# Whole-row loads cast by GpSimd, and single tail banks, in a block-sparse attention and feed-forward kernel

## The chip, the cores and the metric

The kernel runs on one core of a Trainium2 chip. The metric is the device time of one execution in microseconds (us); lower is better. The core has a matrix engine (TensorE, PE in the profile, with its weight loads as PEld), VectorE (DVE), ScalarE (ACT), GpSimd (POOL) and SyncE (SP), and 16 DMA engines that all queues share. SBUF is the memory that the engines work in, PSUM the one that TensorE writes, divided into banks. The granted clock is the share of TensorE's full clock that the profile shows. Kernels are compared with the kernel before as it ran in the same rounds on the same chip.

## The reference, cut to what matters

```python
# q, k, v: [4 batches, 8 heads, 768 tokens, 64] fp32; sampled_blocks: [24, 3]
scores = (q @ k.T) / sqrt(64)
mask   = |block_i - block_j| <= 1, or a first/last block, or a sampled block   # blocks of 32 tokens
attn   = softmax(where(mask, scores, -1e9))
x      = (attn @ v) -> [3072, 512]
xn     = x / sqrt(mean(x*x) + 1e-6) * rms_g
g      = xn @ w_gate                  # [3072, 1536]
out    = (g * sigmoid(g) * (xn @ w_val)) @ w_out      # [3072, 512] fp32
```

## The kernel before

Work is cut into 12 chunks of 256 tokens, three to a batch. Each chunk has an attention part (scores `s_`, exponential and mask product `pt`, output product `o_`) and a feed-forward part (`gp`, `vp` or the tail's `gv`, then `th`, `uu`, `hp`, `yp`). A small list scheduler in the kernel's Python (`Plan`) decides in which order each engine's instructions are written. It is static: once written, an engine runs its instructions in that order, and a time such as `after=60.0` is a hint for the ordering, never a wait on the chip.

K, Q and V of batches 1 to 3 are loaded by GpSimd in slices of one column group, cast from fp32 to bf16 on the way, and laid out so that a DMA transpose can take them:

```python
def load_c(b, i, c):                                   # 128 KB, c = 0..5, K and Q
    ...
    nc.gpsimd.dma_start(
        out=flat[:, c * DM:(c + 1) * DM].rearrange("p (h d) -> p h d", h=H),
        in_=src[b, :, :, c * D:(c + 1) * D])
...                                                    # in the plan, for each c:
nc.gpsimd.dma_start(out=va[b % 2][:, :, c, 0:D], in_=vv4[b, :, :, c, :])
```

GpSimd also computes the normaliser `rs` of each chunk, on which VectorE's scaling of `x` waits, and from there the transposes `xn`, which SyncE issues as DMA transposes for most chunks:

```python
def rstd(ch):
    rs = work.tile([P, 2], FP32, name="rs", tag="rs")
    nc.gpsimd.tensor_scalar(out=rs, in0=mss[ch], scalar1=1e-6, scalar2=None, op0=ALU.add)
    nc.gpsimd.tensor_tensor(out=rs, in0=rs, in1=nhalf, op=ALU.pow)
...
def x_dma(ch, qt):
    ...
    nc.sync.dma_start_transpose(out=xns[ch][:, :, qt * P:(qt + 1) * P], in_=x2s[ch, qt])
```

The mask is applied by a VectorE product whose two inputs both lie in SBUF:

```python
def mask_(t):
    ...
    nc.vector.tensor_tensor(out=pv, in0=pv,
        in1=m.unsqueeze(1).to_broadcast([P, 2, 2 * CQ]), op=ALU.mult)
```

At the end, when no scores are left, the feed-forward borrows the scores' PSUM tiles. One tile of two banks then holds gate and value of a pair together:

```python
def product(w, u, fp, name, half):
    if WIDE(u, fp):
        if (u, fp) not in wide:
            wide[u, fp] = ps_s.tile([P, 2, 512], FP32, name="gv", tag="s")
        pp = wide[u, fp][:, 0 if name == "gp" else 1]
    ...
```

The softmax here doesn't subtract the row's maximum and nothing guards it: scores larger than these inputs give would overflow.

Of the kernel before, what the change touches and what calls it, by code (L numbers as in the profile page):

```python
# [8 lines left out]
FP32 = mybir.dt.float32  # L9
# [6 lines left out]
HOLD = 41.978  # L16
SOFT = 0.0051
LEAD = 29
SPEED = 1.0
PRIO = {'av': 4, 'e': 6, 'g': -5, 'h': -6, 'm': 16, 'mk': -2, 'mt': 4, 'on': -2, 'rs': 21, 's': 3, 'sc': 2, 'sq': 18, 't': 4, 'th': -1, 'uu': -5, 'v': 4, 'x': -2, 'xt': -6, 'y': 7, 'yo': 7}  # L20


class Plan:
# [24 lines left out]
    def run(self, log=None):  # L48
        self.free = free = {e: 0.0 for e in ("PE", "ACT", "DVE", "POOL", "SP")}
        free.update(DVE=4.6, POOL=4.5, ACT=1.5)  # L50
# [4 lines left out]
        dma_free = 14.4  # L55
# [77 lines left out]
def kernel(  # L133
# [13 lines left out]
    P = 128  # L147
# [22 lines left out]
    ps_s = ctx.enter_context(tc.tile_pool(name="ps_s", bufs=2, space=bass.MemoryType.PSUM))  # L170
    ps_o = ctx.enter_context(tc.tile_pool(name="ps_o", bufs=1, space=bass.MemoryType.PSUM))
    ps_f = ctx.enter_context(tc.tile_pool(name="ps_f", bufs=3, space=bass.MemoryType.PSUM))

# [12 lines left out]
    for name, n in (("s", 2), ("o", 1), ("f", 3), ("pt", 4), ("x1", 2), ("x2", 3), ("xn", 3),  # L186
                    ("hp", 2), ("th", 3), ("uu", 3), ("yo", 3), ("qk", 2), ("raw", 1)):
        plan.pool(name, n)
# [26 lines left out]
    def load_c(b, i, c):  # L215
        raw_tiles(b)
        src, t = ((qv, qraw), (kv, kraw))[i]
        flat = t[b].rearrange("p h w -> p (h w)")
        nc.gpsimd.dma_start(  # L219
            out=flat[:, c * DM:(c + 1) * DM].rearrange("p (h d) -> p h d", h=H),  # L220
            in_=src[b, :, :, c * D:(c + 1) * D])
# [10 lines left out]
    load_q(2, 8, 0, 2)  # L232
    jb = const.tile([32, 2 * 32 + 1], I32, name="jb")
    nc.gpsimd.iota(jb[:, 0:32], pattern=[[1, 32]], base=0, channel_multiplier=0)
    nc.gpsimd.iota(jb[:, 32:64], pattern=[[1, 32]], base=0, channel_multiplier=-1)
    nc.gpsimd.iota(jb[:, 64:65], pattern=[[1, 1]], base=0, channel_multiplier=1)
    load_k(2, 4)
    load_k(4, 8)
# [10 lines left out]
    vraw = raw.tile([P, H, NC * D], FP32, name="vraw")  # L249
    for lo in (0, 4):  # L250
        nc.gpsimd.memset(vraw[:, lo:lo + 4, 0:1], 0.0)
        nc.sync.dma_start(out=vraw[:, lo:lo + 4, :], in_=vv[0, :, lo:lo + 4, :])
    gB = const.tile([P, DM], FP32, name="gB")
    nc.sync.dma_start(
        out=gB, in_=moe_rms_g.rearrange("(o f) -> o f", o=1).to_broadcast([P, DM]))
    warm = fbank("warm")
    for _ in range(8):
        nc.tensor.matmul(out=warm, lhsT=idle[:, 0:P], rhs=idle, start=True, stop=True)
# [15 lines left out]
    for lo in (0, 64):  # L274
        nc.vector.tensor_copy(out=R[:, lo:lo + 32], in_=ident[0:32, 0:32])
    jbf = const.tile([32, 2 * 32 + 1], FP32, name="jbf")
    nc.vector.tensor_copy(out=jbf, in_=jb)
    near = const.tile([32, 32], FP32, name="near")
    nc.vector.tensor_tensor(
        out=near, in0=jbf[:, 32:64], in1=jbf[:, 32:64], op=ALU.mult)  # L280
    edge = const.tile([32, 2], FP32, name="edge")
    nc.vector.tensor_scalar(
        out=edge[:, 0:1], in0=jbf[:, 64:65], scalar1=0.0, scalar2=None, op0=ALU.is_equal)
    nc.vector.scalar_tensor_tensor(
        out=edge[:, 1:2], in0=jbf[:, 64:65], scalar=NB - 1.0, in1=edge[:, 0:1],
        op0=ALU.is_equal, op1=ALU.max)
    nc.vector.tensor_scalar(
        out=Bm[:, 0:NB], in0=near[:, 0:NB], scalar1=1.0, scalar2=edge[:, 1:2],
        op0=ALU.is_le, op1=ALU.max)
    nc.vector.memset(Bm[:, 0:1], 1.0)  # L290
    nc.vector.memset(Bm[:, NB - 1:NB], 1.0)
    samp_f = const.tile([32, NRND], FP32, name="samp_f")
    nc.vector.tensor_copy(out=samp_f[0:NB, :], in_=samp_i[0:NB, 0:2 * NRND:2])
    for r in range(NRND):
        nc.vector.scalar_tensor_tensor(
            out=Bm[0:NB, 0:NB], in0=jbf[0:NB, 0:NB], scalar=samp_f[0:NB, r:r + 1],
            in1=Bm[0:NB, 0:NB], op0=ALU.is_equal, op1=ALU.max)
    nc.vector.tensor_copy(out=Bm[0:NB, 64:64 + NB], in_=Bm[0:NB, 0:NB])
# [14 lines left out]
    K_AT = {0: 0.0, 1: 7.4, 2: 10.5, 3: 10.5}  # L313
    V_AT = (12.6, 14.7)

    def cast_first(e, i):
        src, dst = ((qf, qraw[0][:, 0:2, 0:2 * D]), (kf, kraw[0][:, 0:2, :]))[i]
        (nc.scalar.copy if e == "ACT" else nc.vector.tensor_copy)(out=dst, in_=src)

    plan.add("cast0", {"DVE": dve1(256), "ACT": act(256)}, lambda e: cast_first(e, 0), after=3.2,  # L320
             prio=0)
    plan.add("cast1", {"DVE": 0.55, "ACT": act(768)}, lambda e: cast_first(e, 1), after=3.4,
             prio=0)
    plan.add("qrest", {"POOL": 0.8}, lambda e: load_q(0, 8, 2, 6), dma=4.2, prio=0, after=4.5)
    for half in range(2):
        for nm, dst, src in (("wg", wg, wgv), ("wv", wv, wvv)):
            plan.add(
                f"{nm}{half}", {"POOL": 0.8},
                lambda e, d=dst, s=src, h=half: nc.gpsimd.dma_start(
                    out=d[:, :, h * HF:(h + 1) * HF], in_=s[:, :, h * HF:(h + 1) * HF]),  # L330
                dma=3.8, prio=half, after=5.0,
                deps=[">wg0", ">wv0"] if half else [">qrest"])
    plan.add("wo", {"POOL": 0.9}, lambda e: nc.gpsimd.dma_start(
        out=wo, in_=moe_w_out.rearrange("(c p) f -> p c f", p=P)), dma=7.5, prio=2, deps=[">wg1", ">wv1"])
    for i in range(2):
        plan.add(f"one{i}", {"POOL": 0.2}, lambda e, i=i: nc.gpsimd.memset(
            va[i][:, :, :, D:D + 2], 1.0), prio=1, after=7.0)
    for h2 in range(2):
        plan.add(f"va0_{h2}", {"POOL": 1.6}, lambda e, h2=h2: nc.gpsimd.tensor_copy(
            out=va[0][:, 4 * h2:4 * h2 + 4, :, 0:D],  # L340
            in_=vraw[:, 4 * h2:4 * h2 + 4, :].rearrange("p h (c d) -> p h c d", c=NC)),
            deps=["one0"], prio=2 + h2, after=V_AT[h2])

# [25 lines left out]
    TP = [(pr, i, c0, c1) for pr in range(NP) for i, c0, c1 in ((0, 0, 2), (1, 0, NC), (0, 2, NC))]  # L369
    for pr, i, c0, c1 in TP:  # L370
        n = f"{pr}_{i}_{c0}"
        plan.add(f"t{n}", {"PE": 0.04 * 2 * (c1 - c0)},
                 lambda e, pr=pr, i=i, c0=c0, c1=c1: transposes(pr, i, c0, c1),
                 acq=["f"], mode="t", prio=4 if c0 else 0, after=0.0 if c0 else K_AT[pr], lat=0.2,
                 deps=["qrest"] if c0 else [f"cast{i}"] if pr == 0 else [])
        plan.add(f"e{n}", {"DVE": dve2(P * (c1 - c0)) + 0.05, "ACT": act(P * (c1 - c0))},
                 lambda e, pr=pr, i=i, c0=c0, c1=c1: evac_qk(e, pr, i, c0, c1),
                 deps=[f"t{n}"], rel=["f"], prio=0)
# [61 lines left out]
    for i in range(2):  # L440
        plan.add(f"kr{i}", {"PE": 0.3}, lambda e, i=i: key_rows(i), acq=["f"], mode="m",
                 prio=0, after=3.6, lat=0.2)
        plan.add(f"kc{i}", {"DVE": dve1(384), "ACT": act(384)}, lambda e, i=i: key_copy(e, i),
                 deps=[f"kr{i}"], rel=["f"], prio=0)
    for ic in range(NIC):
        plan.add(f"mq{ic}", {"PE": 0.3}, lambda e, ic=ic: mask_query(ic), acq=["f"], mode="m",
                 prio=0, after=QAT[ic], lat=0.2)
# [12 lines left out]
    for b in range(1, B):  # L460
        plan.add(f"rawq{b}", {"SP": 0.0}, lambda e: None, acq=["raw"], lat=0.0, prio=0,
                 deps=[f"raw{b - 1}"] + ([">wo"] if b == 1 else []))
        prev = None
        for i, c0, c1 in KT:
            for c in range(c0, c1):
                plan.add(f"l{b}_{i}_{c}", {"POOL": 0.9},
                         lambda e, b=b, c=c, i=i: load_c(b, i, c),
                         deps=[f"rawq{b}"] + ([">" + prev] if prev else []), dma=2.05, prio=20 + b)
                prev = f"l{b}_{i}_{c}"
        for c in range(NC):  # L470
            plan.add(f"vl{b}_{c}", {"POOL": 0.9}, lambda e, b=b, c=c: nc.gpsimd.dma_start(  # L471
                out=va[b % 2][:, :, c, 0:D], in_=vv4[b, :, :, c, :]),
                deps=[">" + prev] + ([f"one{b % 2}"] if b == 1 else [])
                + ([f"av{(b - 2) * NIC + NIC - 1}_{NP - 1}_2"] if b >= 2 else []),
                dma=2.05, prio=20 + b)
# [3 lines left out]
        for i, c0, c1 in KT:  # L479
            plan.add(f"dt{b}_{i}_{c0}", {"SP": 0.3 + 1.25 * (c1 - c0)},  # L480
                     lambda e, b=b, i=i, c0=c0, c1=c1: transposes_dma(b, i, c0, c1),
                     deps=[f"qk{b}"] + ([">" + prev] if prev else []) + [f"l{b}_{i}_{c}" for c in range(c0, c1)], lat=2.5, prio=1)
# [130 lines left out]
    for run in runs:  # L613
        i = TILES.index(run[0])
        deps = set()
        for ch, pr, j2 in run:
            b, ic = divmod(ch, NIC)
            if b == 0:
                deps |= {f"e{pr}_0_{0 if ic == 0 else 2}", f"e{pr}_1_0"}
# [17 lines left out]
    for ch, pr, j2 in TILES:  # L637
# [13 lines left out]
        if b == 0:  # L651
            deps.append(f"va0_{pr // 2}")
        else:
            deps += [f"vl{b}_{c}" for c in (2 * j2, 2 * j2 + 1)]
# [42 lines left out]
    def product(w, u, fp, name, half):  # L697
        if WIDE(u, fp):
            if (u, fp) not in wide:
                wide[u, fp] = ps_s.tile([P, 2, 512], FP32, name="gv", tag="s")  # L700
            pp = wide[u, fp][:, 0 if name == "gp" else 1]
# [54 lines left out]
    for u in range(NCH):  # L756
        for f in range(NFP):
# [4 lines left out]
            elif u:  # L762
                deps.append(f">v{u - 1}_{NFP - 1}f")
            if f == AHEAD and u:
# [3 lines left out]
                     deps=deps, acq=["s" if WIDE(u, f) else "f"], **w)  # L768
# [5 lines left out]
                     deps=[f"th{u}_{f}"], acq=["uu"], rel=["th"] if WIDE(u, f) else ["f", "th"], prio=2)  # L774
            plan.add(f"v{u}_{f}a", {"PE": pe(CQ, KC)}, lambda e, u=u, f=f: product(wv, u, f, "vp", 0),
                     deps=[f">g{u}_{f}", f"wv{half}"], acq=[] if WIDE(u, f) else ["f"], **w)
# [4 lines left out]
                     acq=["hp"] if f == 0 else [], rel=["s" if WIDE(u, f) else "f", "uu"], prio=2)  # L781
# [53 lines left out]
```

## Time and profile before

| | before |
|---|---|
| median time (3 runs) | 319.47 us (319.18 to 319.92) |
| span of the profiled run, granted TensorE clock | 318.3 us, 0.983 |
| TensorE / VectorE / ScalarE / GpSimd busy | 294.2 / 229.4 / 213.2 / 70.9 us |

The page's table of busy time, kernel before: engine, busy us, share of the span, and the number of instructions.

```profile
PE 294.2 (92%) x3337; PEld 206.2 (65%) x3359; DVE 229.4 (72%) x439; ACT 213.2 (67%) x300; POOL 70.9 (22%) x102
```

TensorE is busy 92% of the time, so time can be won only where it stands still or runs slowly. The waits of TensorE before: what waited, which line's result it waited for, us in total, how often, and the longest.

```profile
PE mp L426 <- DVE uu L719: 7.4, 1, 7.4
PE gv L709 <- ACT th L715: 5.5, 8, 0.7
```

There are two kinds of hole: one wait of 7.4 us, and eight short ones in the tail, where the value matmuls stop for the tanh of the gate that shares their tile. VectorE, for whose `uu` the long one waits, itself waited up to 7.9 us for `rs` from GpSimd (VectorE's waits before, same columns):

```profile
DVE x L582 <- POOL rs L577: 14.7, 10, 7.9
```

The timeline of GpSimd tells the reason. The columns are start, duration, engine, line, operation, output and input, count, and in brackets how long the engine idled before and what ended that.

```profile
43.26 1.74 POOL L219 DMA_DIRECT2D qb<-in_q_dram  x2 [6.46 <-DMA wo<-in_moe_w_out_dram]
45.43 2.63 POOL L219 DMA_DIRECT2D qb<-in_q_dram  x3 [0.43 <-issue]
48.03 4.40 POOL L471 DMA_DIRECT2D va<-in_v_dram  x5
52.64 0.88 POOL L471 DMA_DIRECT2D va<-in_v_dram  x1 [0.20 <-issue]
53.59 0.22 POOL L575 TENSOR_SCALAR rs<-ms 128x2 f32<-128x2 f32 x1
```

GpSimd stood 6.46 us for the load of `wo` to land, then issued five `qb` and six `va` loads, and only then came to `rs`. The stage table of the kernel before gives the busy us of each engine in stretches of 4 us, then the granted clock of TensorE, the share of the DMA engines and GB/s.

```profile
core 0: us, PE busy (x) PEld busy (x) DVE busy (x) ACT busy (x) POOL busy (x), PEclk, DMA share, GB/s
48.00:52.00 4.00, 0.64 (x6) 0.42 (x5) 0.00 (x0) 1.34 (x2) 4.00 (x6) 0.93 2.45 155
52.00:56.00 4.00, 0.00 (x0) 0.00 (x0) 1.36 (x3) 0.00 (x0) 2.25 (x4) 0.50 2.81 148
56.00:60.00 4.00, 3.96 (x27) 2.62 (x28) 3.19 (x7) 2.51 (x3) 0.00 (x0) 0.50 1.03 97
```

TensorE did nothing from 52 to 56 us, and then worked at half the clock. The Trainium skill ("TensorE: Matmul & The Clock Gate", Part 1: The HAM clock gate) says that an idle window of about 3.4 us halves the clock and a busy one of the same length restores it; this trace agrees roughly: the wait began near 48.6 us, the clock was 0.50 from about 51.5 us, some 3 us later, and until about 61.7 us, 5.7 us after work had resumed at 56.0.

Two more lines of the kernel before serve for comparison later: the mask products as a group (busy us, mean ns of one, idle time before them), and the landing times of the `xn` transposes issued between 60 and 125 us.

```profile
L532 DVE TENSOR_TENSOR pt<-pt,Mk 128x1024 bf16<-128x1024 bf16 x132 | 87.2, 684 | 6.0 <-ACT pt L525 6.0
```

```profile
DMA to landing us min/median/max: 2.4/5.3/6.7
```

### The profile page before, as it was taken

Reading aid. Unit: us, or ns where it says so; the run is one execution under the profiler, and the core shown is the slowest. Engines: PE = TensorE matmul, PEld = TensorE weight load, DVE = VectorE, ACT = ScalarE, POOL = GpSimd, SP = SyncE. Lnnn points to the kernel's source line nnn. Section 1 sums busy time; section 2 is a strip of 40 time slices with the busy share of each in tenths; the row PEclk is TensorE's granted clock in tenths of the full one; section 3 lists DMA queues with packets and bytes.
Section 4 is the critical chain, followed back from the end, with each engine's and each line's share of the span. In section 5 each row is a group of like instructions: output and inputs, shape, how many; then the busy total and the mean of one; then the engine's idle time right before and its main releaser. Section 6 shows DMA issues by size and latency. Waiting matters only on the chain.

```text
span 318.3 us, 7937 instructions
## 1 busy us (share of the span) xinstructions
PE 294.2 (92%) x3337; PEld 206.2 (65%) x3359; DVE 229.4 (72%) x439; ACT 213.2 (67%) x300; POOL 70.9 (22%) x102
## 2 busy tenths in 40 slices
PE   7998991999899999999999999999999999997975
PEld 2675780577658667757867757848758758675552
DVE  6239981786859978987986977887978969745151
ACT  4789991465778887888876976967867866332221
POOL 9326258007094109570010000100100100100000
PEclk9999997699999999999999999999999999999999
DMA  7999999869999989999921020020020020010101
GB/s 124 252 233 210 208 163 153 103 104 111 136 102 149 132 150 114 149 111 131 166 50 52 2 69 35 0 68 35 0 69 35 16 81 7 30 38 0 68 0 66
DMA packets 97655, 29.61 MB, mean 93 GB/s; under 512 B 87380, under 2 KB 94548, under 8 KB 97620
## 3 DMA queue, kind: packets, MB, share of 16 engines
q0 software_dynamic: 62448, 13.11, 50.9%
q1 hardware_dynamic: 34756, 15.74, 25.5%
q8 instruction: 26, 0.43, 0.6%
q10 hardware_dynamic: 416, 0.26, 0.3%
q14 instruction: 9, 0.07, 0.1%
HBM read 28.57 MB, written 6.29 MB: 110 GB/s over the span
## 4 chain that ended last, share of the span: by engine, by line
PE 68%; DMA 11%; POOL 7%; DVE 6%; ACT 4%; issue 3%; POOLq 0%; ACTq 0%; DVEq 0%
PE yp L736 17%; PE gp L709 14%; PE vp L709 14%; DMA wo<-in_moe_w_out_dram 11%; PE gv L709 5%; ACT junk L569 2%; POOL va L471 2%; ACT th L715 2%; DVE hp L726 2%; DVE x L582 2%; POOL qb L219 1%; DVE uu L719 1%; DVE pt L532 1%; POOL rs L577 1%; POOL qb L209 1%
## 5 line engine op out<-in xcount | busy, mean ns | idle before, releaser
L532 DVE TENSOR_TENSOR pt<-pt,Mk 128x1024 bf16<-128x1024 bf16 x132 | 87.2, 684 | 6.0 <-ACT pt L525 6.0
L709 PE MATMUL vp<-xn,wv 128*128 128x256 bf16 x512 | 69.8, 275 | 0.0
L736 PE MATMUL yp<-wo,hp 128*128 128x512 bf16 x266 | 67.6, 382 | 1.3 <-DVE hp L726 0.2
L709 PE MATMUL gp<-xn,wg 128*128 128x256 bf16 x512 | 66.4, 273 | 1.1 <-DVE hp L726 1.1
L709 PEld LDWEIGHTS <-wg 128*128 128x128 bf16 x576 | 56.1, 98 | 10.3 <-issue 1.7
L709 PEld LDWEIGHTS <-wv 128*128 128x128 bf16 x576 | 52.8, 98 | 13.9 <-issue 8.3
L715 ACT ACTIVATE th<-gp 128x512 bf16<-128x512 f32 x64 | 38.3, 598 | 28.0 <-PE gp L709 26.2
L546 PEld LDWEIGHTS <-pt 128*128 128x128 bf16 x1152 | 43.3, 98 | 19.6 <-issue 9.2
L719 DVE SCALAR_TENSOR_TENSOR uu<-th,gp 128x512 bf16<-128x512 bf16 x64 | 43.6, 682 | 14.5 <-ACT th L715 14.1
L726 DVE TENSOR_TENSOR hp<-uu,vp 128x512 bf16<-128x512 bf16 x64 | 43.6, 682 | 4.0 <-PE vp L709 1.9
L736 PEld LDWEIGHTS <-hp 128*128 128x128 bf16 x288 | 25.9, 98 | 25.8 <-issue 3.2
L575 POOL TENSOR_SCALAR rs<-ms 128x2 f32<-128x2 f32 x12 | 2.8, 230 | 168.1 <-ACT junk L569 168.0
L510 PEld LDWEIGHTS <-qkT 64*128 64x128 bf16 x576 | 23.9, 96 | 20.7 <-issue 16.4
L753 ACT ACTIVATE yo<-yp 128x512 f32<-128x512 f32 x23 | 13.8, 598 | 24.6 <-PE yp L736 24.5
L582 DVE SCALAR_TENSOR_TENSOR x<-x,rs,gB 128x512 bf16<-128x512 f32 x24 | 17.6, 748 | 14.8 <-POOL rs L577 14.7
L219 POOL DMA_DIRECT2D qb<-in_q_dram x18 | 15.8, 911 | 19.9 <-DMA qkT<-qb 9.3
L471 POOL DMA_DIRECT2D va<-in_v_dram x18 | 15.9, 923 | 4.7 <-PE o__2395 L546 4.5
L219 POOL DMA_DIRECT2D kb<-in_k_dram x18 | 16.0, 912 | 1.4 <-DMA wg<-in_moe_w_gate_dram 1.4
L719 DVE SCALAR_TENSOR_TENSOR uu<-th,gv 128x512 bf16<-128x512 bf16 x8 | 5.5, 687 | 14.9 <-PE gv L709 14.9
L569 ACT ACTIVATE junk<-x 128x512 bf16<-128x512 f32 x24 | 15.0, 628 | 1.9 <-DVE x L560 1.8
L709 PE MATMUL gv<-xn,wv 128*128 128x256 bf16 x64 | 9.6, 272 | 5.5 <-ACT th L715 5.5
L715 ACT ACTIVATE th<-gv 128x512 bf16<-128x512 f32 x8 | 4.8, 597 | 14.3 <-PE gv L709 14.3
(509 smaller groups left out, 386.2 us busy)
## 6 DMA issues: line engine op xcount, KB each, us to landing
out_dram<-yo SPq DMA_DIRECT2D x23, 256.0 KB, 2.1
kb<-in_k_dram POOLq DMA_DIRECT2D x18, 128.0 KB, 7.6
qb<-in_q_dram POOLq DMA_DIRECT2D x18, 128.0 KB, 6.9
va<-in_v_dram POOLq DMA_DIRECT2D x18, 128.0 KB, 6.8
vraw<-in_v_dram SPq DMA_DIRECT2D x2, 768.0 KB, 12.0
wg<-in_moe_w_gate_dram POOLq DMA_DIRECT2D x2, 768.0 KB, 21.4
wv<-in_moe_w_val_dram POOLq DMA_DIRECT2D x2, 768.0 KB, 24.4
wo<-in_moe_w_out_dram POOLq DMA_DIRECT2D x1, 1536.0 KB, 34.2
```

The costliest lines, as they stand in the source:

```text
L219: nc.gpsimd.dma_start(out=flat[:, c * DM:(c + 1) * DM].rearrange("p (h d) -> p h d", h=H), in_=src[b, :, :, c * D:(c + 1) * D])
L471: plan.add(f"vl{b}_{c}", {"POOL": 0.9}, lambda e, b=b, c=c: nc.gpsimd.dma_start(out=va[b % 2][:, :, c, 0:D], in_=vv4[b, :, :, c, :]), deps ...
L510: nc.tensor.matmul(out=s_[:, e, jj * CQ:(jj + 1) * CQ], lhsT=x[rows, 1, 2 * j2 + jj, pr, :], rhs=x[rows, 0, 2 * ic:2 * ic + 2, pr, :], sta ...
L532: nc.vector.tensor_tensor(out=pv, in0=pv, in1=m.unsqueeze(1).to_broadcast([P, 2, 2 * CQ]), op=ALU.mult)
L546: nc.tensor.matmul(out=o_[:, qt, e, 0:D + 1], lhsT=pt[:, j2, e, jj * CQ + qt * P:jj * CQ + (qt + 1) * P], rhs=va[(ch // NIC) % 2][:, 2 * p ...
L569: nc.scalar.activation(out=junk, in_=x1s[ch][:, qt].rearrange("p h d -> p (h d)"), func=AF.Square, scale=float(DM) ** -0.5, accum_out=mss[ ...
L582: nc.vector.scalar_tensor_tensor(out=x2s[ch, qt], in0=x1s[ch][:, qt].rearrange("p h d -> p (h d)"), scalar=mss[ch][:, qt:qt + 1], in1=gB, ...
L709: nc.tensor.matmul(out=pp[:, half * CQ:(half + 1) * CQ], lhsT=w[:, c, f * P:(f + 1) * P], rhs=xns[u][:, c, :], start=(c == 0), stop=(c == ...
L715: nc.scalar.activation(out=ths[u, fp], in_=gst[u, fp, "gp"], func=AF.Tanh, scale=0.5)
L719: nc.vector.scalar_tensor_tensor(out=uus[u, fp], in0=ths.pop((u, fp)), scalar=1.0, in1=gst.pop((u, fp, "gp")), op0=ALU.add, op1=ALU.mult)
L726: nc.vector.tensor_tensor(out=hps[u][:, 2 * fp:2 * fp + 2, :].rearrange("p f t -> p (f t)"), in0=uus.pop((u, fp)), in1=gst.pop((u, fp, "vp ...
L736: nc.tensor.matmul(out=yst[u, t], lhsT=hps[u][:, f, t * P:(t + 1) * P], rhs=wo[:, f, :], start=(f == 0), stop=(f == NF - 1))
```

## The change

The intent is to shorten GpSimd's queue and to free the tail:

- K, Q and V of batches 1 to 3 are loaded as whole rows, one plain fp32 load of 1.5 MB each, into a staging tile. GpSimd then casts them from there into the layout for the DMA transposes. So 54 casting loads become nine plain loads and 48 casts. (Batch 0's V goes the same way, in two loads and four casts.)
- V of batch 0 is loaded in the same GpSimd queue, before the rest of Q and the weights.
- The tail takes four single banks from a new pool in place of the two double tiles.
- The scheduler's constants and priorities were tuned again for the new plan, and the first steps rearranged (seven warm-up matmuls in place of eight, the mask's preparation put into the plan).

```diff
-    def load_c(b, i, c):
+    def load_stage(b, i):
+        stages[b, i] = raw.tile([P, H, NC * D], FP32, name="stage", tag="stage", bufs=2)
+        if b:
+            nc.gpsimd.dma_start(out=stages[b, i], in_=(qv, kv, vv)[i][b])
+
+    def cast_c(b, i, c):
         raw_tiles(b)
...
-        nc.gpsimd.dma_start(
+        nc.gpsimd.tensor_copy(
             out=flat[:, c * DM:(c + 1) * DM].rearrange("p (h d) -> p h d", h=H),
-            in_=src[b, :, :, c * D:(c + 1) * D])
+            in_=stages[b, i][:, :, c * D:(c + 1) * D])
+
+    def cast_v(b, pr):
+        nc.gpsimd.tensor_copy(
+            out=va[b % 2][:, 2 * pr:2 * pr + 2, :, 0:D],
+            in_=stages[b, 2][:, 2 * pr:2 * pr + 2, :].rearrange("p h (c d) -> p h c d", c=NC))
...
+        for i in (1, 0, 2):                            # K, Q, V of batch b
+            swdge(f"l{b}_{i}", lambda b=b, i=i: load_stage(b, i), 4.4,
+                  [">wo"] if (b, i) == (1, 1) else [">" + last], 20 + b, acq=["stage"],
+                  after=0.0 if b == 1 else 60.0 * b - 20.0)
...
     def product(w, u, fp, name, half):
-        if WIDE(u, fp):
-            if (u, fp) not in wide:
-                wide[u, fp] = ps_s.tile([P, 2, 512], FP32, name="gv", tag="s")
-            pp = wide[u, fp][:, 0 if name == "gp" else 1]
+        if WIDE(u, fp) and half == 0:
+            if not wide:
+                s_stack.close()
+                wide[0] = ctx.enter_context(
+                    tc.tile_pool(name="ps_t", bufs=4, space=bass.MemoryType.PSUM))
+            pp = wide[0].tile([P, 512], FP32, name="gv", tag="t")
```

## The prediction

> **What bounds it now.** TensorE: the busy table has it busy 294 of 318.3 us, VectorE 229, ScalarE 213, GpSimd 71. From 90 to 270 us the stage table shows TensorE 98-100% busy at full clock; chunks there repeat every 22.8 us, which is what their matmuls take. Time can only come from holes:
>
> 1. *The hole at 48.65 us.* The waits view gives TensorE one wait of 7.4 us. The timeline names the cause: GpSimd's in-order queue. The normaliser's `rs` for chunk 1 (its squares were ready at 46.0) runs at 53.6, behind six `qb` and six `va` load issues of 0.88 us each, which themselves waited 6.5 us for the `wo` load to land at 43.3. VectorE waits 7.9 us for `rs`. Then the granted clock is 0.50 from about 51.5 to 61.5 us. The Trainium skill ("TensorE: Matmul & The Clock Gate", Part 1) says about 3.4 us of idleness halves the clock; this trace agrees. Some 5.5 us of matmuls ran at half rate: 2.5-3 us more. Hole total about 10 us.
> 2. *The tail.* Eight waits of 0.69 us, `gv` for ScalarE `th`: gate and value share one two-bank tile, so the value matmuls stop until the tanh of the gate has ended. 5.5 us.
> 3. *Start.* To the first FFN matmul at 29.65 us, about 3 us more than its matmuls; ScalarE's exponentials (0.91 us apart) bind there.
> 4. *End:* last output, about 4 us.
>
> **What the change does.** Per later batch, 18 casting loads of 128 KB (0.91 us of GpSimd each, 16.4 us) become 3 plain whole-row loads (2.7 us) plus 16 GpSimd casts. The 128x1536 cast took 1.47 us, so I estimate 0.5 us for 128x512 and 0.75 us for 128x768: 9 us a batch. In the order of the changed kernel, chunk 1's `rs` stands before all casts of batch 1, and only the K and Q loads stand before it, whose queue slots freed early. So hole 1 and its half clock go: about -10 us. The tail takes four single banks: gate and value no longer block one another, and the bank of the pair after next is free before it is wanted (gate end + 0.8 + 0.7 us against 2.6 us): -5.5 us.
>
> Loads: `wo` should still land near 43; it read 3.1 MB in 7.4 us, so K of batch 1 lands at about 47.5, Q at 52, casts end near 57, transposes near 60. Summing matmul durations in the new order, the first scores of batch 1 are wanted near 65 us: just in time. V before the weights helps the first output products by 1-3 us, but the exponentials bind: -0.5 us or so.
>
> **Cost.** "SBUF — State Buffer" (two separate sides) says a GpSimd operation and a VectorE one with two SBUF inputs exclude each other. The mask products (132 of 0.66 us) are such; no run here shows it yet. 27 us of casts may delay VectorE by up to 12 us in sum; with 14% slack on VectorE from 100 to 180 us I allow TensorE +2 us.
>
> Sum: 319.5 - 10 - 5.5 - 0.5 + 2 = 303.5 us; range 298.5 to 309. Chances: faster by over 2% 0.95, within 2% 0.04, slower 0.01.
>
> **Signs.** Right: no TensorE wait above 3 us and clock 1.00 after 15 us; no `gv` wait for `th`; GpSimd issues 9 batch loads; chunk period still 22.8 us. Casts of `kb` clearly over 0.5 us beside mask products, or masks over 0.68 us: the port lock is real.
>
> **What would make it wrong.** Batch 1's K/Q arriving after 65 us, so that the fixed order stalls TensorE there; casts stretched to 1 us or more; `rs` of chunk 2 or 7 held behind casts that wait for a load; the lengthened period.

## The result, and the profile after

| | before (same rounds) | after |
|---|---|---|
| median time (4 runs each) | 319.7 us (319.18 to 320.01) | 314.89 us (314.4 to 316.11) |
| ratio after to before | | 0.9857, 95% interval 0.9825 to 0.9889 |
| span of the profiled run, clock | 318.3 us, 0.983 | 312.6 us, 0.989 |

A ratio here is the mean time of one kernel's fast runs over that of the other's of the same rounds, so it is not quite the ratio of the medians quoted beside it. Where a gain or a cost is told in us below, it is a difference of two such ratios times 319.5 us, which takes out small differences between the rounds. By that measure the change gained 4.6 us, and 16 had been forecast.

The waits of TensorE after, in the same columns as before:

```profile
PE gp L757 <- DMA xn<-x: 4.6, 1, 4.6
PE o__1059 L592 <- DVE pt L578: 3.1, 2, 2.7
PE o__342 L592 <- POOL va L234: 1.9, 1, 1.9
PE o__2062 L592 <- DVE pt L578: 1.4, 1, 1.4
```

Both old kinds of wait are gone: no `mp` wait of 7 us, no `gv` wait. In their place stand waits that the kernel before did not have: 4.6 us for a DMA transpose, and 3.1, 1.9 and 1.4 us for a mask product, a V cast and another mask product. The timeline of GpSimd after shows that the cure of the old hole worked as planned.

```profile
46.52 0.22 POOL L621 TENSOR_SCALAR rs<-ms 128x2 f32<-128x2 f32 x1 [20.78 <-ACT junk L615]
...
47.48 4.78 POOL L229 CAST kb<-stage 128x512 bf16<-128x512 f32 x6
52.56 0.95 POOL L224 DMA_DIRECT2D stage<-in_v_dram  x1 [0.30 <-POOL kb L229]
53.51 3.84 POOL L229 CAST qb<-stage 128x512 bf16<-128x512 f32 x6
```

`rs` of chunk 1 now runs at 46.52 us instead of 53.59. But it is followed by casts, twelve in nearly unbroken runs. The timeline of VectorE after, beside the second of these runs:

```profile
53.51 5.00 DVE L578 TENSOR_TENSOR pt<-pt,Mk 128x1024 bf16<-128x1024 bf16 x3
```

Three mask products took 5.00 us there; one of them alone took 3.38 us, and 0.68 us is what a mask product takes undisturbed. This one was the first of the three; it started in the same instant as the first `qb` cast. The next stage table is of the kernel after, with the columns of the one before.

```profile
52.00:56.00 4.00, 2.24 (x30) 1.21 (x27) 4.00 (x4) 2.51 (x3) 3.70 (x7) 1.00 0.77 154
56.00:60.00 4.00, 3.05 (x19) 1.45 (x20) 3.96 (x7) 0.00 (x1) 1.36 (x2) 0.57 0.99 346
```

From 52 to 56 us VectorE was busy all of the time, waiting inside its mask products, and TensorE 2.24 us. The half clock came back as well, for a shorter time: 0.57 on average from 56 to 60 us. As groups, the mask products and the casts after, in the columns of the group view:

```profile
L578 DVE TENSOR_TENSOR pt<-pt,Mk 128x1024 bf16<-128x1024 bf16 x132 | 94.5, 742 | 3.9 <-ACT pt L571 3.8
...
L234 POOL CAST va<-stage 128x768 bf16<-128x768 f32 x16 | 14.3, 928 | 15.8 <-DMA stage<-in_v_dram 15.8
L229 POOL CAST kb<-stage 128x512 bf16<-128x512 f32 x18 | 13.9, 812 | 5.8 <-DMA stage<-in_k_dram 5.8
...
L229 POOL CAST qb<-stage 128x512 bf16<-128x512 f32 x18 | 12.4, 734 | 0.0
```

The mask products grew by 7.3 us in sum. The casts, which take 0.61 us (128x512) where nothing disturbs them, average 0.81 and 0.73 us: each side delays the other.

The second new hole, of 4.6 us, ends at 107.86 us. Two whole-row loads of batch 2 were issued just beside the two `xn` transposes of chunk 3, which SyncE issued at 93.90 and 96.02. This is GpSimd's timeline after:

```profile
93.01 0.95 POOL L224 DMA_DIRECT2D stage<-in_k_dram  x1
93.96 0.88 POOL L224 DMA_DIRECT2D stage<-in_q_dram  x1
```

And this is the view of the DMA queues of the kernel after from 92 to 108 us. The first line gives the packets of the loads' queue, its MB and the share of the 16 engines' time; the others give issues, KB each, and median us from issue to landing.

```profile
q0 software_dynamic: 736, 3.15, 63.6%
...
stage<-in_k_dram POOLq DMA_DIRECT2D x1, 1536.0 KB, 7.8
stage<-in_q_dram POOLq DMA_DIRECT2D x1, 1536.0 KB, 12.4
out_dram<-yo SPq DMA_DIRECT2D x1, 256.0 KB, 12.1
xn<-x SPq DMA_TRANSPOSE x2, 13.1
```

The first of the two transposes took 13.1 us to land (the profile shows no landing of the second; TensorE's wait for both ended 11.8 us after its issue). 2.4 us is the shortest in this trace, and an output store beside them took 12.1 us. In the kernel before, the `xn` transposes issued between 60 and 125 us landed in at most 6.7 us, this longest one beside slice loads of K; chunk 3's own, issued as the last V slices landed, took 3.5 and 2.4 us. But small pieces do not make every transpose quick. From 92 to 108 us of the kernel before, two K transposes, each three times as large as one of `xn`, ran beside slice loads with packets of 1.34 MB / 10607 = 0.13 KB:

```profile
q0 software_dynamic: 10607, 1.34, 141.9%
...
qkT<-kb SPq DMA_TRANSPOSE x2, 12.9
```

A load packet of the kernel after averages 3.15 MB / 736 = 4.3 KB, and the 16 engines moved up to 419 GB/s in this window, 26 GB/s each, so a load packet holds an engine for about 0.16 us. A pair of transposes and a store alone, in a quiet stretch, show 1104 packets under 512 B, some 34 for each transpose and engine. An estimate from these numbers: if each small packet lets one large one pass, 34 x 0.16 = 5.5 us for a transpose and 11 us for a pair, near the 13.1 measured. The Trainium skill ("DMA: Bandwidth & Descriptors", Queues, rings and completion order) states that each DMA engine goes round its queues packet by packet; this estimate agrees in size with the trace, which doesn't show single turns, and d2_slices below does not bear it out.

How far each kernel is ahead can be read from when a given piece of work starts:

| start of | before | after | lead |
|---|---|---|---|
| first feed-forward matmul | 29.65 | 28.74 | 0.9 |
| first scores of batch 1 | 78.09 | 70.81 | 7.3 |
| 73rd score group (batch 2 begins) | 136.06 | 139.59 | -3.5 |
| last score group | 266.47 | 269.89 | -3.4 |
| end of the matmuls | 314.43 | 309.08 | 5.4 |

Single milestones also reflect the changed order (scores may run earlier or later against the feed-forward), but the pattern is plain: a gain up to about 100 us, lost again near 105 us, nothing between 140 and 266 us, and a gain in the tail.

### The profile page after: what moved, and what is told of

The parts are those of the page before. It is cut to its first block, busy times and chain, and to the rows that moved or that the text cites. A ratio compares the mean times of both kernels' runs of the same rounds, so it can differ in the third digit from the quotient of the medians.

```text
span 312.6 us, 7944 instructions
## 1 busy us (share of the span) xinstructions
PE 291.9 (93%) x3358; PEld 204.3 (65%) x3358; DVE 238.3 (76%) x439; ACT 214.4 (69%) x302; POOL 70.7 (23%) x108
## 4 chain that ended last, share of the span: by engine, by line
PE 60%; DVE 16%; DMA 8%; ACT 7%; POOL 5%; issue 4%; POOLq 0%; ACTq 0%; DVEq 0%
PE yp L784 14%; PE gp L757 13%; PE vp L757 12%; DVE pt L578 6%; PE gv L757 4%; DVE x L628 4%; DMA stage<-in_v_dram 4%; DMA xn<-x 4%; ACT junk L615 3%; ACT pt L571 3%; DVE uu L767 2%; DVE hp L774 2%; POOL rs L623 2%; DVE x L606 2%; ACT th L763 1%
## 5 line engine op out<-in xcount | busy, mean ns | idle before, releaser
L578 DVE TENSOR_TENSOR pt<-pt,Mk 128x1024 bf16<-128x1024 bf16 x132 | 94.5, 742 | 3.9 <-ACT pt L571 3.8
L784 PE MATMUL yp<-wo,hp 128*128 128x512 bf16 x288 | 71.5, 384 | 0.7 <-DVE hp L774 0.7
L757 PE MATMUL gp<-xn,wg 128*128 128x256 bf16 x512 | 67.3, 275 | 4.6 <-DMA xn<-x 4.6
L592 PEld LDWEIGHTS <-pt 128*128 128x128 bf16 x1152 | 45.9, 98 | 28.3 <-DVE pt L578 11.1
L757 PEld LDWEIGHTS <-wv 128*128 128x128 bf16 x576 | 51.8, 97 | 6.5 <-issue 1.1
L628 DVE SCALAR_TENSOR_TENSOR x<-x,rs,gB 128x512 bf16<-128x512 f32 x24 | 19.2, 840 | 12.7 <-POOL rs L623 12.6
L234 POOL CAST va<-stage 128x768 bf16<-128x768 f32 x16 | 14.3, 928 | 15.8 <-DMA stage<-in_v_dram 15.8
L229 POOL CAST kb<-stage 128x512 bf16<-128x512 f32 x18 | 13.9, 812 | 5.8 <-DMA stage<-in_k_dram 5.8
L229 POOL CAST qb<-stage 128x512 bf16<-128x512 f32 x18 | 12.4, 734 | 0.0
L623 POOL TENSOR_TENSOR rs<-rs,nhalf 128x2 f32<-128x2 f32 x12 | 8.6, 715 | 1.0
```

The lines of the kernel that those rows point to most:

```text
L229: nc.gpsimd.tensor_copy(out=flat[:, c * DM:(c + 1) * DM].rearrange("p (h d) -> p h d", h=H), in_=stages[b, i][:, :, c * D:(c + 1) * D])
L578: nc.vector.tensor_tensor(out=pv, in0=pv, in1=m.unsqueeze(1).to_broadcast([P, 2, 2 * CQ]), op=ALU.mult)
L592: nc.tensor.matmul(out=o_[:, qt, e, 0:D + 1], lhsT=pt[:, j2, e, jj * CQ + qt * P:jj * CQ + (qt + 1) * P], rhs=va[(ch // NIC) % 2][:, 2 * p ...
L628: nc.vector.scalar_tensor_tensor(out=x2s[ch, qt], in0=x1s[ch][:, qt].rearrange("p h d -> p (h d)"), scalar=mss[ch][:, qt:qt + 1], in1=gB, ...
L757: nc.tensor.matmul(out=pp[:, half * CQ:(half + 1) * CQ], lhsT=w[:, c, f * P:(f + 1) * P], rhs=xns[u][:, c, :], start=(c == 0), stop=(c == ...
L784: nc.tensor.matmul(out=yst[u, t], lhsT=hps[u][:, f, t * P:(t + 1) * P], rhs=wo[:, f, :], start=(f == 0), stop=(f == NF - 1))
```

## The experiments

The theory on reading the traces was that the change did remove both old costs, and brought two of its own: **the port cost**, mask products held while GpSimd casts, and **the transposes' cost**, `xn` held behind the large loads. The rivals were that the old gains had been overrated, that the order of the new plan by itself was worse, and, against the port cost, that the mask products were only late because their exponentials were.

### t1_tail: the tail banks alone, on the kernel before

```diff
+    s_stack = ExitStack()
+    ps_s = s_stack.enter_context(tc.tile_pool(name="ps_s", bufs=2, ...))
...
-        if WIDE(u, fp):
-            if (u, fp) not in wide:
-                wide[u, fp] = ps_s.tile([P, 2, 512], FP32, name="gv", tag="s")
+        if WIDE(u, fp) and half == 0:
+            if not wide:
+                s_stack.close()
+                wide[0] = ctx.enter_context(tc.tile_pool(name="ps_t", bufs=4, ...))
+            pp = wide[0].tile([P, 512], FP32, name="gv", tag="t")
```

> The kernel before with nothing but the tail's banks changed: four single banks from a new pool in place of two two-bank tiles; every engine keeps its order. Theory (the tail part of the change is sound and independent of the rest): the eight TensorE waits of 0.69 us for the tanh vanish, time falls by 5.0 to 5.6 us, to about 314.3 us. Rival (the chain tanh, product, product would bind next, or the banks collide): some waits come back in another form and the gain is under 3 us.

Measured: 312.26 us median (311.58 to 313.48), ratio 0.9796 (0.9761 to 0.9832), so 6.5 us gained, a little more than expected. Every engine's order is that of the kernel before. The waits of TensorE:

```profile
PE mp L427 <- DVE uu L722: 7.3, 1, 7.3
PE gp L712 <- DMA xn<-x: 1.3, 1, 1.3
```

The `gv` waits are gone and the 7 us wait is still there, as it should be. The eight waits of 0.69 us are 5.5 us of idle time, but a stop costs more than its idle time. In the tail of the kernel before, matmuls of one bank start some 0.11 us apart and last 0.27 us each, overlapping (four of them take 0.60 us). At a stop the last one runs out before the idle time counts, so the next starts 0.27 + 0.69 = 0.96 us after it, 0.85 us later than usual. 8 x 0.85 = 6.8 us is an estimate that fits the gain. This one part of the change gained more than the whole did.

### h1_rs_first and h2_rs_tail: the old hole cured without the new loads

The hole before came from the order in GpSimd's queue, so it may be cured by the order: Q and V of batch 1 are loaded after `rs` of chunk 1. Nothing else moves. h2 adds the tail banks of t1.

```diff
-                         deps=[f"rawq{b}"] + ([">" + prev] if prev else []), dma=2.05, prio=20 + b)
+                         deps=[f"rawq{b}"] + ([">" + prev] if prev else [])
+                         + ([">rs1"] if (b, i) == (1, 0) else []), dma=2.05, prio=20 + b)
```

> The kernel before with one dependency added: GpSimd issues the Q and V loads of batch 1 after the two normaliser operations of chunk 1 instead of before them; nothing else moves on any engine. It takes away the old hole alone, with no cast, no whole-row load and the old tail. Theory (the hole of 7.4 us and its half clock cost what the prediction said, and the gain was spent elsewhere): TensorE's 7.4 us wait goes, time falls by 8 to 11 us to about 309.5 us, although the Q and V loads start 3 us later. Rival (the hole only held time that the next limit, Q and K of batch 1, would have taken anyway): a new wait of several us appears near 60 to 75 us and time falls by less than 5 us.

Measured: 314.2 us median (311.65 to 314.89), ratio 0.9809 (0.9762 to 0.9856), a gain of 6.1 us, and less than the 8 to 11 us that had been expected. Its four runs differ by more than the others': 314.88 and 314.89 us at a granted clock of 0.981, 313.51 at 0.995 and 311.65 at 0.999. The profiled run is one of the two longest. Its stage table (same columns):

```profile
28.00:32.00 4.00, 3.88 (x36) 2.03 (x32) 3.43 (x6) 2.97 (x5) 1.98 (x4) 0.57 1.16 212
...
50.00:60.00 10.00, 9.57 (x118) 5.94 (x114) 8.97 (x18) 7.23 (x10) 8.88 (x11) 1.00 1.85 145
...
70.00:80.00 10.00, 7.71 (x62) 5.62 (x60) 5.42 (x10) 5.38 (x7) 5.33 (x6) 0.83 1.77 187
```

From 50 to 60 us the hole is gone (TensorE 9.57 of 10 us at full clock). TensorE's order is that of the kernel before, so the starts of the same matmuls in the two timelines tell how far one run is ahead of the other: between 48 and 62 us of the kernel before, h1 gained 9.0 us. Two places took some back. From 28 to 32 us, which the edit does not touch, this run was granted 0.57, where the run of the kernel before had 1.00, and lost 1.3 us; why it was throttled there was not found out. And at 70 us TensorE waited 2.3 us for a transpose of Q, whose loads the edit puts later, and ran at half clock after it (0.83 on average from 70 to 80 us): 3.3 us lost. This is the rival of the expectation, though smaller than the hole. The run with the highest clock, 311.65 us, is 8.2 us below the median before.

> The kernel before with both that dependency and the four tail banks, and nothing else of the change. If the two gains add (8 to 11 us and the 6.8 us measured for the tail), 301 to 304 us: below both kernels, and proof that the new load path as a whole costs more than it gives. If the old hole's removal is masked, 308 us or more.

Measured: 304.82 us median (304.54 to 305.12), ratio 0.953 (0.9512 to 0.9548), all four runs at a clock of 0.999 or 1.0, and the result is right; 301 to 304 us had been expected. It is the fastest correct kernel here: 15.0 us below before, and some 10 us below after. Against t1 the hole's cure is worth 8.5 us. The longest waits of TensorE in it:

```profile
PE s__1346 L512 <- DMA qkT<-qb: 2.0, 1, 2.0
PE tq L360 <- DMA kb<-in_k_dram: 1.2, 1, 1.2
```

So the two old costs were real, 6.5 and about 8.5 us, the latter less what the later Q loads cost (the wait of 2.0 us). The rival that the gains had been overrated falls.

### d1_gate: the large loads held back until the transposes have landed

A GpSimd copy of two columns of `xn` stands before the K and Q loads of batches 2 and 3, so that these are issued only when the transposes of chunk 3 (6) are done.

```diff
+    held = const.tile([P, 2], BF16, name="held")
...
     def load_stage(b, i):
         stages[b, i] = raw.tile([P, H, NC * D], FP32, name="stage", tag="stage", bufs=2)
+        if b > 1 and i == 1:
+            ch = {2: 3, 3: 6}[b]
+            nc.gpsimd.tensor_copy(out=held, in_=xns[ch][:, 0, 0:2 * P:P])
```

> The changed kernel with one GpSimd copy of two elements per partition put before the loads of K and Q of batch 2 and of batch 3: it reads the normalised chunk (3 and 6) that the DMA transposes of that moment write, so the loads start only when these have landed. Theory (whole-row loads starve the DMA transposes beside them): the transposes of chunk 3 land in about 2.4 us instead of 13.1, TensorE's wait of 4.6 us for them at 103 us and the half clock after it vanish, time falls by 4.5 to 6.5 us, to about 309 us. Rival (the transposes were late for another reason: the queue of SyncE, or the scaled rows came late): they still land late, time within 1 us of the changed kernel.

Measured: 308.04 us median (307.22 to 308.93), ratio 0.966 (0.9631 to 0.969), 6.3 us below after. GpSimd's timeline of d1_gate, and the landing of its `xn` transposes issued between 88 and 112 us:

```profile
97.27 0.18 POOL L226 COPY held<-xn 128x2 bf16<-128x2 bf16 x1 [5.73 <-DMA xn<-x]
97.75 0.95 POOL L228 DMA_DIRECT2D stage<-in_k_dram  x1 [0.30 <-issue]
98.70 0.88 POOL L228 DMA_DIRECT2D stage<-in_q_dram  x1
```

```profile
DMA to landing us min/median/max: 2.4/2.4/2.4
```

The transposes land in 2.4 us, the wait of 4.6 us is gone together with the half clock that had followed it (the clock is 1.00 throughout from 100 to 114 us), and TensorE's order is exactly that of after. The loads go out 4.7 us later and nothing waits for them. The longest mask product is still 3.38 us (sum 95.5 us), as the two costs should be separate. Part of the gain in the profiled run is luck of the start: the wait for the first V cast was 0.5 instead of 1.9 us, and by the starts of the same matmuls it was 1.5 us ahead of after before 20 us, and gained 6.2 us more between 99.6 and 113.5 us of after. The runs' interval leaves the cost at about 5 to 7 us.

### d2_slices: the same bytes in smaller pieces

K and Q of batches 2 and 3 are loaded plain, but in six pieces of 256-byte rows each.

```diff
-            nc.gpsimd.dma_start(out=stages[b, i], in_=(qv, kv, vv)[i][b])
+            for c in range(NC if b > 1 and i < 2 else 0):
+                nc.gpsimd.dma_start(
+                    out=stages[b, i][:, :, c * D:(c + 1) * D],
+                    in_=(qv, kv, vv)[i][b][:, :, c * D:(c + 1) * D])
+            if not (b > 1 and i < 2):
+                nc.gpsimd.dma_start(out=stages[b, i], in_=(qv, kv, vv)[i][b])
```

> The changed kernel with K and Q of batches 2 and 3 loaded at the same moment in six plain pieces of 256-byte rows each instead of whole rows: the same bytes, no cast, packets about 16 times smaller. Theory A (a transpose's packet waits for one packet of the load each turn, so large packets starve it): the transposes of chunk 3 land in 4 to 8 us, TensorE's wait at 103 us falls below 1 us, time 4 to 6 us below the changed kernel. Theory B (it is the volume of bytes ahead that counts): they land in 11 us or more and the wait stays above 3 us.

Measured: 312.04 us median (311.41 to 312.64), ratio 0.9755 (0.973 to 0.9781), 3.3 us below after. The waits of TensorE and the landing of the transposes issued between 90 and 112 us:

```profile
PE gp L762 <- DMA xn<-x: 1.9, 1, 1.9
```

```profile
DMA to landing us min/median/max: 6.5/6.5/6.5
```

The first transpose lands in 6.5 us, half of 13.1, and the wait falls from 4.6 to 1.9 us; a wait under 1 us and a gain of 4 to 6 us had been expected. But the edit did not make the packets 16 times smaller. The loads' queue of d2_slices from 92 to 108 us:

```profile
q0 software_dynamic: 618, 2.08, 62.7%
```

That is 2.08 MB / 618 = 3.4 KB a packet, against 4.3 KB in after. So this run does not test the size of a packet. What changed is the pace: twelve issues from 94 to 107 us in place of two within 2 us, and 2.08 MB moved in this window in place of 3.15. The shorter landing speaks for the pace, or the bytes that stand in the queue; the estimate by turns, which still gives 2 x 34 x 0.13 = 9 us for a pair at 3.4 KB a packet, does not explain it.

### c2_fill and x1_gate_fill: GpSimd writes the same tiles without reading SBUF

The casts of batches 1 to 3 become memsets of the same outputs. The result is wrong (relative error 1.17 in c2); the order and the writes stay, the reads of SBUF go.

```diff
-        nc.gpsimd.tensor_copy(
-            out=flat[:, c * DM:(c + 1) * DM].rearrange("p (h d) -> p h d", h=H),
-            in_=stages[b, i][:, :, c * D:(c + 1) * D])
+        nc.gpsimd.memset(flat[:, c * DM:(c + 1) * DM], 0.01)
...                                                    # and cast_v likewise
```

> Wrong result on purpose: the changed kernel with each GpSimd cast of batches 1 to 3 replaced by a GpSimd memset of the same output, so GpSimd writes as before but reads no SBUF; loads, transposes and all orders stay. Theory (casts read SBUF through the port pair that the mask products' second input needs): no mask product above 0.75 us in the whole run, sum of the 132 mask products back from 94.5 to about 87.3 us, the waits of TensorE for mask products (5.5 us in all) nearly gone, time 3 to 6 us below the changed kernel. Rival (DMA writes of whole fp32 rows into SBUF slow VectorE): mask products as long as in the changed kernel, time unchanged.

Measured: 308.52 us median (307.45 to 309.1), ratio 0.9681 (0.9653 to 0.9709), 5.6 us below after. The groups of mask products and of the memsets in c2_fill:

```profile
L582 DVE TENSOR_TENSOR pt<-pt,Mk 128x1024 bf16<-128x1024 bf16 x132 | 87.1, 685 | 3.6 <-ACT pt L575 3.4
...
L231 POOL MEMSET kb<- 128x512 bf16 x18 | 8.6, 526 | 0.0
```

The sum of the mask products is that of the kernel before again (87.1 and 87.2 us), and the longest is 0.693 us although the memsets, 0.53 to 0.76 us each, run in the same unbroken rows beside them. No wait for a mask product over 0.3 us is left; the wait for `xn` is still 4.5 us. So a busy GpSimd does no harm to the mask products, and neither late exponentials nor the whole-row loads, which still run, are the reason; the GpSimd instruction that reads SBUF is. The Trainium skill ("SBUF — State Buffer", SBUF: two separate sides) says just this: a pair of ports shared by the two engines is an exclusive lock, which a VectorE operation with two SBUF inputs needs only against a GpSimd operation that reads SBUF. The traces agree. A caveat: a memset does not wait for a load to land and is a little shorter than a cast, so 5.6 us is an upper bound of the lock's own cost rather than its exact size. Where it was lost can be read from the starts of the same matmuls (TensorE's order is that of after): c2_fill gains 4.9 us between 48.0 and 60.1 us of after, beside the casts of batch 1, 1.5 us between 113.5 and 126.2 (batch 2) and 0.6 us between 173.1 and 193.3 (batch 3).

> Wrong result on purpose: the gate of the loads and the memsets in place of the casts together, in the changed kernel. If the two new costs are separate, their gains add: about 6.9 us for the loads and 6.4 us for the port give 301 to 303 us. If they are one cost seen twice, it stays near 307 us.

Measured, with the gate of d1 as well: 302.63 us median (300.59 to 305.06), ratio 0.9487 (0.944 to 0.9534). That is 11.8 us below after, and the two cures alone gave 6.3 + 5.6 = 11.9. The two costs add up, so they are two.

### c3_gap, x2_gate_gap and x3_gate_long: can the casts be made to let the masks through?

c3 puts a GpSimd memset of one element after each cast, on the kernel after. x2 does so on the gated kernel d1. x3 makes the memset as long as a cast (128x512, into a scratch tile).

```diff
+    gap = const.tile([P, 2], FP32, name="gap")        # x3: [P, 512], BF16
...
     def cast_c(b, i, c):
         ...
+        nc.gpsimd.memset(gap[:, 0:1], 0.0)            # x3: the whole tile; the same in cast_v for b > 0
```

> The changed kernel with a one-element GpSimd memset after each cast of batches 1 to 3. Theory (the run of casts holds the shared SBUF port from the first to the last, because each cast starts before the one before it has ended): if the memset breaks the run, no mask product is longer than about 1.3 us (one cast plus itself), TensorE's wait of 2.7 us at 54 us shrinks below 1 us, time falls by 2 to 4 us. If the port is held all the same, the mask product of 3.4 us stays and time is unchanged or up to 1 us longer. Rival (mask products are slow for another reason than the casts): unchanged.

Measured: 313.9 us median (313.79 to 314.03), ratio 0.9844 (0.9821 to 0.9866), 0.4 us below after; 2 to 4 us had been expected. The longest mask product beside the casts of batch 1 fell from 3.38 to 1.71 us, but one near 190 us took 2.88 us and the sum was 95.5 us.

> The gated kernel (308.04 us) with a one-element GpSimd memset after each cast. If the gap really lets VectorE's mask products in and the small gain of the gap on the ungated kernel (about 1 us) was only hidden because PE then waited for the starved transposes in any case: 304.5 to 306.5 us, and no PE wait for a mask over 1.2 us. If the short gap only moves the blocked stretches to later masks, as the mask sum of 95.5 us in both suggested: 307 to 308.5 us, with at least one mask product still over 2.5 us.

Measured: 308.37 us median (307.56 to 308.91), ratio 0.9644 (0.9608 to 0.968). Against the gate alone (0.966) that is no difference that the intervals would bear out. The longest mask product is 2.89 us and the sum 96.0 us. So no gain in the total had been hidden behind the wait for the transposes.

> The gated kernel with a memset of a scratch 128x512 tile (about 0.54 us, a GpSimd instruction that reads nothing) after each cast. If what blocks a mask product is the unbroken run of casts, every mask can slip in during a memset: longest mask 1.3 us or less (0.69 plus one cast of 0.61), sum of masks 88 to 91 us. The casts of one operand then take about 1.2 us per slice instead of 0.64, so q of batch 1 is done some 3 us later; it may be wanted earlier than that. Time 304 to 307 us if the lock is what costs, 308 or more if the later operands cost as much as the lock gave. If instead a mask is held by the casts' number and not by their being back to back, masks over 2.5 us remain.

Measured: 307.92 us median (307.45 to 308.12), ratio 0.9636 (0.9607 to 0.9665), again within the intervals of the gate alone. The groups in x3_gate_long:

```profile
L586 DVE TENSOR_TENSOR pt<-pt,Mk 128x1024 bf16<-128x1024 bf16 x132 | 94.9, 746 | 2.1 <-ACT pt L579 2.1
...
L237 POOL MEMSET gap<- 128x512 bf16 x36 | 18.7, 519 | 0.0
...
L234 POOL CAST kb<-stage 128x512 bf16<-128x512 f32 x18 | 11.8, 655 | 8.6 <-DMA stage<-in_k_dram 8.6
```

The forecast of at most 1.3 us for the longest mask product and a sum of 88 to 91 us was missed: the longest is 1.57 us, and the sum is 94.9 us. The long holds were broken up and more products were held for a shorter time each; over the whole kernel the products took 7.7 us more than in the kernel before, where d1's took 8.3 us more. The `kb` casts did come out shorter, 0.65 us in place of 0.81. Spacing the casts shares the hold-ups more evenly and takes next to nothing from their sum. Why the sum stays so constant wasn't tried further.

The medians do not show that the spacing helps where VectorE has no slack. The wait for the mask product of batch 1, 3.1 us in after and in d1, is in x3_gate_long:

```profile
PE o__1064 L600 <- DVE pt L586: 0.5, 1, 0.5
```

By the starts of the same matmuls, c3, x2 and x3 gained 2.5, 2.5 and 3.1 us between 53.9 and 60.1 us of after, where d1 gained 0.3. Part of it was lost again: about 1 us in c3 and x2 near 195 us, 0.9 us in x3 by 74 us. And before 20 us, which no edit touches, d1's profiled run was 1.5 us ahead of after, x3's 0.6 us behind. With starts that differ by 2 us and four runs each, a gain of 1 to 2 us in total is neither shown nor excluded.

## Why the prediction was wrong

The forecast was 303.5 us with 298.5 to 309 as its range; 314.89 us was measured. Its gains were right, and its costs were not. The chain of runs, by ratios: from before to h2 (both old costs cured, old loads) -15.0 us; from h2 to x1 (the new plan with both new costs taken out) -1.4 us, within overlapping intervals; from x1 to after +11.8 us. The sum is -4.6 us. The changed kernel without the two new costs took 302.63 us (x1, with a wrong result); the forecast without its +2 us for the lock was 301.5 us.

- **The hole at 48.65 us, "about -10 us".** Right in mechanism: `rs` runs at 46.52 us and the 7.4 us wait is gone. The hole is worth about 8.5 us (h2 against t1), a little less than forecast: where it stood h1 gained 9.0 us, but its cure there puts Q later, with a wait of 2.0 to 2.3 us.
- **The tail, "-5.5 us".** Right in mechanism, a little small: 6.5 us (t1), because a stop costs about 0.85 us and the waits view shows 0.69 of it.
- **The start, "-0.5 us".** The first feed-forward matmul came 0.9 us earlier in the profiled run. But it starts at 27.2 to 29.3 us in the eight traces of the new plan and at 28.8 to 29.75 us in the four of the old one, so half a microsecond can't be told from luck.
- **"With 14% slack on VectorE from 100 to 180 us I allow TensorE +2 us."** This is the first step that failed. The lock is real, as the signs had named: casts over 0.5 us and mask products over 0.68. The sum of the mask products' delays, 7.3 us, even stayed under the 12 us allowed. But the slack was taken from the wrong stage. The casts of batch 1 fall where VectorE has none: from 52 to 56 us it was busy 4.00 of 4.00 us, and TensorE stood 2.7 us and then ran at half clock. Removing the reads gained 5.6 us. In the timelines of the profiled runs (c2_fill's is its fastest) 4.9 us stand beside the casts of batch 1 and 2.1 us beside those of batches 2 and 3, for which +2 us was about right. In the late steady stage there was slack indeed: TensorE is busy all of 40 us between 200 and 240 us.
- **The estimate of 0.5 and 0.75 us for a cast.** 0.61 and 0.82 us undisturbed, 0.73 to 0.93 on average. Casts of 1 us or more had been named as a danger; some reached 1.07 us (128x512) and 1.29 us (128x768).
- **"No TensorE wait above 3 us and clock 1.00 after 15 us."** Wrong. There is one of 4.6 us and a pair with one of 2.7 us, and half clock from 56.4 to 59.8 and from 107.6 to 111.0 us. (The chunk period, another sign, held: from the 73rd to the last score group it is 130.4 us before and 130.3 after.) The 4.6 us wait is the second step that failed, by leaving something out: the prediction asked when the large loads would land, and never what else shares their engines. The gate alone gave back 6.3 us.
- **"Batch 1's K/Q: just in time."** Right: no TensorE wait for `qkT` stands in the profile after. "GpSimd issues 9 batch loads" and "no `gv` wait" were right too.

What stays open: the exact share of the lock in the 5.6 us, since the memsets also don't wait for loads; how the loads hold the transposes up (packet size was not tested, pace only in d2); whether spaced casts gain 1 to 2 us; and why the profiled run of h1 was granted less clock from 28 to 32 us.

## What to carry to other kernels

When a change swaps many small transfers for a few large ones, ask which small transfers that an engine waits for share the DMA engines at that moment, and hold the large ones until those have landed: here a two-column copy as a gate gave 6.3 us. When work moves to GpSimd, cost its reads of SBUF against VectorE's two-input operations in the stage where they will stand together, not with the average slack. And before replacing a slow queue, try its order: moving twelve loads behind two small instructions, with the tail's banks, was 10 us faster than the whole rework.

## What the Trainium skill lacked or had wrong

- "SBUF — State Buffer", SBUF: two separate sides. It says that whoever starts first holds the shared ports for the whole instruction. The runs show more than that: in an unbroken run of `qb` casts of 0.64 us (six in 3.84 us), one mask product was held for 3.38 us, several casts long. The page doesn't say that a waiting VectorE operation may lose again at each boundary.
- The same page, in its summary of rules, advises only to schedule whichever operation is off the critical path. The runs found no remedy for the sum: with gaps of 0.1 us or of 0.52 us after each cast the mask products took 96.0 and 94.9 us, against 95.5 without gaps and 87.1 beside GpSimd instructions that read nothing. But the longest hold fell, from 3.38 us to 2.89 and 1.57 us.
- "DMA: Bandwidth & Descriptors", Bandwidth and Rules for kernel authors. The advice to batch transfers to 1 MiB or more, and the remark that a transpose next to ordinary DMAs needs nothing (said of correctness, which held here), name no price for the transposes. Here they landed in 13.1 us beside two loads of 1.5 MB, in 6.5 us beside the same bytes in slices spread over a longer time (packets of 3.4 KB in place of 4.3), and in 2.4 us alone.
- No page has the number for a stop of TensorE behind a bank shared by gate and value: a wait of 0.69 us cost about 0.85 us by estimate, and eight of them 6.5 us as measured.
